# Moving pieces of preparation to other steps and reordering the closing products of a routed attention and GLU kernel

## The chip, the cores and the metric

The kernel runs on one core of one Trainium2 chip. Its five engines work side by side: PE (matmuls), DVE (elementwise work and reductions), ACT (activations), POOL (elementwise work) and SP (which only issues DMAs here). The metric is the device time of one execution in microseconds (us); less is better. All times below are in us unless ns is written.

## The reference, cut to what matters

```python
# 4 batches, 8 heads, 768 tokens, head size 64, 16 centroids per head
q_assign = argmax(q_n @ c_n.T); k_assign = argmax(k_n @ c_n.T)     # nearest centroid
mask = q_assign[:, None] == k_assign[None, :]
attn = softmax(where(mask, q @ k.T / 8, -1e9))
x = (attn @ v) with the heads side by side                         # 3072 x 512
out = (sigmoid(x @ w_gate) * (x @ w_val)) @ w_out                  # 512 -> 1536 -> 512
```

Each query attends only to keys that chose the same centroid. The attention's output goes through a gated feed-forward block.

## The kernel before, in words

**Steps.** The attention runs in 384 steps. A step is one block of 128 keys against 384 queries of one head: one `sc` matmul (line 893), an exponential on ACT (`es`, line 898), and, two steps later for batches 1 to 3, three `av` matmuls (line 916). Batch 1 has steps 96 to 191, batch 2 192 to 287, batch 3 288 to 383. The heads go in pairs, and a pair (b, p) is pair p of batch b. The last pair of a batch is done in two halves of 384 queries: for batch 2 the first half of its last pair takes steps 264 to 275. With it the first 384 tokens of the batch are complete.

**An order written out by hand.** No scheduler moves instructions: each engine executes in the order in which the program issues them. Between the steps, three things are inserted:

- *Feed-forward work* (`ffn_atoms`, line 515, `ffn_run`, line 845): per step as many matmuls as a time budget allows. `g` (line 530) and `v` (line 546) are gate and value products, four matmuls each; `hT` (line 551) on DVE joins them. The output product is made in a Strassen-like form of seven products (`product_out`, line 744). Its matmuls (line 821) alternate between two PSUM banks x and y, and each product's result is added out by DVE (`ob`, line 768) before the bank is used for the next product but one. In order they are known in the trace by their right-hand operands: hT, hT, qheld, kheld, vheld, wo with sum, hT.
- *Preparation of later pairs* (`pair_prep`, line 1451). It splits q and k into high and low halves (`hl`, lines 1458 and 1459), transposes them by DMA (`T<-hl`, line 410), multiplies with the centroids in twelve matmuls (`lg`, line 434), picks the largest on DVE (`lgs`, `mx`, `oh`, lines 449 to 469), transposes the picks by DMA (`ohT`) and copies them into the rows of T that make the mask. `v_sum` (line 324) adds up v over the keys: three adds on DVE (lines 330, 336, 337), a matmul with ones (`vs_ps`, line 341) and a scaling (`sv`, line 346), which the normalisation of the pair needs at its end.
- *Normalisation* (`normalise`, line 366): t and rec on DVE, xp on POOL, then a transposing DMA from SP into `xTb` (line 947), which is the input of `g`.

The table `SCHED` (from line 21) gives the step at which each piece is issued, as an offset to the first step of its pair. `b1p3lg1` is the second head's lg of batch 1, pair 3, whose first step is 168. `b2...` holds for batches 2 and 3 where no `b3p...` entry overrides it: `vs` is the first add of the v sum, `vu` the other two, `vt` the matmul and the scaling, `lg0` and `pk0` the first head's lg and pick. First steps: pair (3,0) 288, pair (3,1) 312.

**PSUM.** The tiles of sc, g, v, lg, vs_ps and o_end take turns in a ring of four banks; a matmul into a bank waits until the bank's former tile has been read.

**The end.** After the last step the second half of batch 3's feed-forward runs alone. `closing` (line 575) makes the output of four blocks of 128 tokens in two such seven-product groups, a and b. `pa(k)` and `pb(k)` are product k of a group, six matmuls of 256 columns (line 594); la and lb are each group's last product. Products 1, 4, 6 and 5 take a bank of their own; product 7 goes on top of 6, and 3 on top of 5, in the same bank, after 6 and 5 have been added out (line 580). For group a these banks are the two fixed output banks, for b ring banks. `last` (line 628) makes the last product in column parts, adds each out, and stores 256 columns of 128 tokens at once (`store`, line 500, on SP's queue).

Of the kernel before, what the change touches and what calls it, by code (L numbers as in the profile page):

```python
# [94 lines left out]
}  # L95


@with_exitstack
def kernel(
# [12 lines left out]
    PE, ACT, DVE, POOL, SP = nc.tensor, nc.scalar, nc.vector, nc.gpsimd, nc.sync  # L112
    B, H, S, D = q.shape
    NCL = centroids.shape[1]
    DM = out.shape[1]
# [45 lines left out]
    def bank(n=512, dt=FP, name="bank"):  # L161
        return ring.tile([128, n], dt, tag="ring", name=name)
# [3 lines left out]
    def out_bank():  # L166
        taken["op"] += 1
        return op.tile([128, DM], FP, tag="o", name="o")
# [94 lines left out]
    HF, HD = NFC // 2, DM // 2  # L263
# [233 lines left out]
    def tok(b, t, f):  # L497
        return HB[b, t // 3][:, HF * f : HF * f + HF, bass.ts(t % 3, 128)]

    def store(src, b, c0, n, m=slice(0, DM)):  # L500
        def f():
            SP.dma_start(
                out=out[b * S : (b + 1) * S].rearrange("(p c) m -> p c m", c=NCH)[
                    :, c0 : c0 + n, m
                ],
                in_=src,
            )

        d_ = SCHED.get("sd", 0)
        if d_ > 0 and b < B - 2:  # L510
            at(step_no[0] + d_, f)
        else:
            f()

    def ffn_atoms(xT, t0, n, b, final=False):
# [55 lines left out]
        if final:  # L571
            return closing(b, gv, sm[(3, 2)], sm[(4, 5)])
        return gv + outs

    def closing(b, gv, ma, mb):

        ac, order = [], []
        plus = lambda dst, a, z: DVE.tensor_tensor(dst, a, z, ALU.add)  # L580

        def pair(m, bk):
            st = {}
            lhs = {
                1: lambda: tok(b, m.t1, 0), 2: lambda: tok(b, m.t1, 1), 4: lambda: tok(b, m.t2, 1),
                6: lambda: m.of[2], 5: lambda: m.of[1], 7: lambda: m.of[3], 3: lambda: m.of[4],
            }
            rhs = {1: B11, 2: B21, 3: B22, 4: T4, 5: T1, 6: T2, 7: T3}
            C = lambda i, j: st["ob"][:, i, HD * j : HD * j + HD]

            def mm(o, k, g, n, start, a=0, z=HD):
                w = lhs[k]()
                for c in range(g, g + n):
                    PE.matmul(  # L594
                        out=o, lhsT=w[:, c, :], rhs=rhs[k][:, c, a:z],
                        start=start and c == 0, stop=c == HF - 1, skip_group_check=True,
                    )

            def product(k, g=0, n=HF):
                def f():  # L600
                    z = {1: "a", 4: "d", 6: "x", 7: "x", 5: "y", 3: "y"}[k]
                    if g == 0 and k in (1, 4, 6, 5):
                        if k == 1:
                            st["ob"] = osp.tile([128, 2, DM], FP, name="ob")
                        st[z] = bk(z)
                    o = st[z][:, 0:HD]
                    mm(o, k, g, n, k not in (7, 3))
                    if g + n < HF:
                        return
                    if k == 1:  # L610
                        ACT.activation(C(0, 0), o, AF.Copy)
                    elif k == 4:
                        plus(C(1, 0), o, C(0, 0))
                    elif k == 6:
                        plus(C(0, 1), o, C(0, 0))
                    elif k == 5:
                        plus(C(1, 1), o, C(0, 0))
                    elif k == 7:
                        plus(C(1, 0), o, C(1, 0))
                        plus(C(1, 1), o, C(1, 1))  # L620
                        store(st["ob"][:, 1:2], b, m.t2, 1)
                    else:
                        plus(C(0, 1), o, C(0, 1))
                        store(st["ob"][:, 0:1, HD:DM], b, m.t1, 1, slice(HD, DM))

                return f

            def last(parts):
                def f():
                    for a, z in parts:  # L630
                        o = bank(z - a, name="o_end")
                        mm(o, 2, 0, HF, True, a, z)
                        plus(st["ob"][:, 0, a:z], o, st["ob"][:, 0, a:z])
                    store(st["ob"][:, 0:1, 0:HD], b, m.t1, 1, slice(0, HD))

                return f

            return product, last

        two = {}  # L640

        def bank_a(z):
            if z in "ad":
                need(*(("wo", i) for i in range(WOP)), *(("wt", i, c) for i in range(4) for c in range(2)))
                two[z] = out_bank()
            return two[{"x": "a", "y": "d"}.get(z, z)]

        pa, la = pair(ma, bank_a)
        pb, lb = pair(mb, lambda z: bank(512, name="o_end"))
        early = [pa(k, g, HF // 2) for k in (1, 4, 6, 5) for g in (0, HF // 2)]  # L650

        def drained(f):
            def g():
                while aside:
                    aside.pop(0)[1]()
                f()

            return g

        early[0] = drained(early[0])  # L660
        atoms = gv[:14]
        for i, x in enumerate(gv[14:]):
            atoms.append(x)
            if i < len(early):
                atoms.append((0.0, early[i]))
        for f in (
            pa(7), pb(1), pb(4), pa(3), pb(6), pb(5), la([(0, HD)]), pb(7), pb(3),
            lb([(0, HD // 2), (HD // 2, HD)]),
        ):
            atoms.append((0.0, f))  # L670
        return atoms
# [280 lines left out]
    def at(i, f):  # L952
        bg.setdefault(max(i, step_no[0] - 0.5), []).append(f)
# [11 lines left out]
    def need(*names):  # L965
        for n in names:
            assert n in done, n
# [361 lines left out]
    a = P[0, 0, 0]  # L1329
# [199 lines left out]
    for b in range(B):  # L1529
        xT = xtp.tile([128, NDC, S], HP, tag="xTb", name="xTb")  # L1530
        key = min(b, 1)
        for i in range(2 if b else NPT):
# [4 lines left out]
            c0, cn = PARTS[i] if b == 0 else (3 * i, 3)  # L1537
            for w in range(1 + (cn > 3)):
                z = cn // (1 + (cn > 3))
# [51 lines left out]
```

## Time and profile before

| what | value |
|---|---|
| median of 3 runs | 322.78 us (322.7 to 324.16) |
| the profiled execution's own time | 323.67 us |
| its span (first to last instruction) | 321.9 us |
| PE's granted clock over the span | 0.999 |
| mean DMA traffic | 140 GB/s |

In a line of the timeline stand the start, the duration, the engine, the line of the kernel, the operation, the output, the input, the shape, and in square brackets how long the engine was idle before and which instruction released it. Lines of the waits give the waiter, the one waited for, the sum, the count and the longest. Lines of the chain give start, duration and the link. SPq and ACTq are the instructions by which SP and ACT issue DMAs; a DMA's line gives its size and the us from issue to landing. Records of matmuls overlap, since each is counted until its data is out.

### The profile page before, as it was taken

What the parts mean: (1) busy time and instruction counts of PE and PEld (TensorE: products, weight loads), DVE (VectorE), ACT (ScalarE), POOL (GpSimd) and SP (SyncE); (2) the same over time, 40 slices, a digit from 0 to 9 for tenths busy, and PEclk for the clock granted to TensorE, in tenths of its full rate; (3) what the DMA queues carried; (4) which work ended last, traced back from release to release, by engine and by line L of the source; (5) the groups of instructions that cost most, each with busy time, mean ns of one, the idle gap of its engine ahead of it and who ended that gap; (6) DMA issues with size and microseconds to landing.
All of it is one profiled execution on the core that took longest, in us unless ns stands there. A gap on an engine that the chain in (4) does not pass through costs nothing.

```text
span 321.9 us, 9181 instructions
## 1 busy us (share of the span) xinstructions
PE 314.6 (98%) x3510; PEld 222.4 (69%) x3510; DVE 224.9 (70%) x598; ACT 231.1 (72%) x521; POOL 108.6 (34%) x145
## 2 busy tenths in 40 slices
PE   7999999999999999999999999999999999999996
PEld 5888666766666666666777687566777688667775
DVE  5799656777787677576878587586767356456666
ACT  6688988787888888877867866778877886332320
POOL 6877464154434365433133333414211111000000
PEclk9999999999999999999999999999999999999999
DMA  7999997738876996978884751942503112200103
GB/s 214 374 256 180 244 171 118 210 75 236 238 113 187 163 238 155 223 172 136 108 219 115 217 113 33 314 110 52 111 2 90 40 26 79 77 2 1 65 2 131
DMA packets 77709, 45.16 MB, mean 140 GB/s; under 512 B 56865, under 2 KB 75105, under 8 KB 77665
## 3 DMA queue, kind: packets, MB, share of 16 engines
q1 hardware_dynamic: 73696, 39.73, 49.7%
q0 software_dynamic: 3680, 4.72, 9.0%
q8 instruction: 27, 0.44, 0.6%
q10 hardware_dynamic: 288, 0.13, 0.2%
q14 instruction: 18, 0.14, 0.2%
HBM read 28.34 MB, written 6.29 MB: 108 GB/s over the span
## 4 chain that ended last, share of the span: by engine, by line
PE 89%; DMA 3%; DVE 3%; issue 2%; POOL 1%; SPq 0%; ACT 0%; POOLq 0%; DVEq 0%
PE g L530 19%; PE v L546 19%; PE sc L893 17%; PE av L916 10%; PE o L821 8%; PE o L684 5%; PE lg L434 2%; PE o_end L594 2%; DMA T<-hl 2%; PE lg L421 1%; PE t_ps L1142 1%; PE o L594 1%; DMA xTb<-xp 1%; PE oh_ps L1202 1%; DMA qraw<-in_q_dram 1%
## 5 line engine op out<-in xcount | busy, mean ns | idle before, releaser
L898 ACT ACTIVATE es<-sc 128x384 f16<-128x384 f32 x384 | 174.3, 492 | 40.6 <-PE sc L893 31.9
L893 PE MATMUL sc<-T 128*128 128x384 f16 x384 | 117.8, 326 | 0.4 <-DVE T L1223 0.4
L916 PEld LDWEIGHTS <-es 128*128 128x128 f16 x1152 | 81.3, 98 | 35.9 <-issue 0.8
L916 PE MATMUL av<-va,es 128*128 128x65 f16 x1152 | 97.6, 194 | 0.0
L551 DVE SCALAR_TENSOR_TENSOR hT<-th,v 128x384 f16<-128x384 f32 x96 | 53.0, 553 | 55.6 <-PE av L916 36.0
L530 PE MATMUL g<-xTb,wg 128*128 128x384 f16 x384 | 78.2, 326 | 0.7 <-DMA xTb<-xp 0.5
L546 PE MATMUL v<-xTb,wv 128*128 128x384 f16 x384 | 78.1, 326 | 0.0
L536 ACT ACTIVATE th<-g 128x384 f32<-128x384 f32 x96 | 47.2, 491 | 35.0 <-PE g L530 15.9
L375 POOL TENSOR_TENSOR xp<-t,rec 128x384 f16<-128x384 f32 (+1 forms) x30 | 21.6, 720 | 101.8 <-DVE rec L372 52.3
L530 PEld LDWEIGHTS <-wg 128*128 128x128 f16 x384 | 37.2, 97 | 19.3 <-issue 0.4
L546 PEld LDWEIGHTS <-wv 128*128 128x128 f16 x384 | 37.4, 98 | 18.6
L893 PEld LDWEIGHTS <-T 128*128 128x128 f16 x384 | 37.1, 97 | 0.6 <-DVE T L1223 0.5
L1459 POOL TENSOR_TENSOR hl<-kraw,hl 128x384 f16<-128x384 f32 x22 | 20.2, 920 | 41.1 <-DVE hl L1458 20.5
L1459 POOL TENSOR_TENSOR hl<-qraw,hl 128x384 f16<-128x384 f32 x22 | 20.9, 950 | 9.8 <-DVE hl L1458 9.8
L768 DVE TENSOR_TENSOR ob<-o,ob 128x256 f32<-128x256 f32 (+1 forms) x35 | 17.8, 523 | 7.6 <-PE o L821 6.8
L370 DVE TENSOR_TENSOR t<-av,sv 128x390 f32<-128x390 f32 (+1 forms) x30 | 14.4, 479 | 9.7 <-PE av L916 7.3
L821 PEld LDWEIGHTS <-sum 128*128 128x128 f16 x168 | 16.4, 98 | 5.2 <-issue 0.8
L684 PE MATMUL o<-wo,hT 128*128 128x512 f16 x72 | 19.9, 379 | 0.0
L821 PE MATMUL o<-wo,hT 128*128 128x256 f16 x126 | 19.8, 272 | 0.0
L449 DVE TENSOR_REDUCE lgs<-lg 128x192 f32<-128x384 f32 x23 | 12.7, 551 | 2.8 <-PE lg L434 2.7
L821 PEld LDWEIGHTS <-hT 128*128 128x128 f16 x126 | 12.2, 97 | 3.4
L322 POOL CAST va<-vraw 128x768 f16<-128x768 f32 x15 | 13.0, 869 | 1.9 <-DMA vraw<-in_v_dram 1.9
(158 smaller groups left out, 340.1 us busy)
## 6 DMA issues: line engine op xcount, KB each, us to landing
vraw<-in_v_dram SPq DMA_DIRECT2D x15, 384.0 KB, 4.9
kraw<-in_k_dram SPq DMA_DIRECT2D x14, 384.0 KB, 4.3
qraw<-in_q_dram SPq DMA_DIRECT2D x12, 384.0 KB, 4.2
out_dram<-ob SPq DMA_DIRECT2D x18, 256.0 KB, 2.4
wg<-in_moe_w_gate_dram POOLq DMA_DIRECT2D x2, 768.0 KB, 9.5
wv<-in_moe_w_val_dram POOLq DMA_DIRECT2D x2, 768.0 KB, 10.3
wo<-in_moe_w_out_dram POOLq DMA_DIRECT2D x2, 768.0 KB, 9.3
T<-ohT SPq DMA_DIRECT2D x44, 24.0 KB, 1.9
```

The source lines that it names most:

```text
L375: (eng or POOL).tensor_tensor(x, t[:, 0:nq, 0:64], bcast(rec[:, 0:nq], 64), ALU.mult)
L530: PE.matmul(out=g[:, 0:n], lhsT=wg[fc // WQ][:, dc, fc % WQ, :], rhs=xT[:, dc, t0 : t0 + n], start=(dc == 0), stop=(dc == NDC - 1),)
L536: ACT.activation(th[:, 0:n], g[:, 0:n], AF.Tanh)
L546: PE.matmul(out=w[:, 0:n], lhsT=wv[fc // WQ][:, dc, fc % WQ, :], rhs=xT[:, dc, t0 : t0 + n], start=(dc == 0), stop=(dc == NDC - 1),)
L551: DVE.scalar_tensor_tensor(HB[b, blk][:, fc, 0:n], st[0][:, 0:n], 1.0, w[:, 0:n], ALU.add, ALU.mult)
L684: PE.matmul(out=o, lhsT=HB[b, blk][:, fc, bass.ts(t, 128)], rhs=wo[fc // WON][:, fc % WON, :], start=(fc == 0), stop=(fc == NFC - 1),)
L768: plus = lambda dst, a, z: DVE.tensor_tensor(dst, a, z, ALU.add)
L821: PE.matmul(out=st[z][:, e], lhsT=a[:, c, :], rhs=rhs[:, c, :], start=start and c + e == 0, stop=c == HF - 1, skip_group_check=True,)
L893: PE.matmul(out=sc.rearrange("p (c t) -> p c t", t=128), lhsT=s["k"], rhs=s["q"], start=True, stop=True,)
L898: ACT.activation(es, sc, AF.Exp, scale=SCALE)
L916: PE.matmul(out=av[:, a0 + s["c0"] + i, :], lhsT=s["es"][:, bass.ts(i, 128)], rhs=VA[b, p][:, e, s["j"], :], start=(first and i == 0 and a ...
L1459: POOL.tensor_tensor(hl[:, :, 64:128], r, hl[:, :, 0:64], ALU.subtract)
```

## The change: five pieces at other steps, another closing order, the last store in two

Pieces of preparation:

| piece | step before | step after |
|---|---|---|
| pair (1,3), second head's lg | 139 | 140 |
| pair (3,0), v sum, first add | 269 | 258 |
| pair (3,0), v sum, other two adds | 271 | 260 |
| pair (3,0), v sum, matmul and scaling | 290 | 279 |
| pair (3,1), first head's lg and pick | 273 | 280 |

In the closing order pb(6), pb(5) and pb(7) go ahead of pa(3) and la. Each column part of a group's last product is stored by itself: for group a there is one part, stored from SP as before; for group b the first 128 columns are stored from SP and the last 128 from ACT's queue.

```diff
-    "b1p3lg1": -29
+    "b1p3lg1": -28
+    "b3p0vs": -30, "b3p0vu": -28, "b3p0vt": -9, "b3p1lg0": -32, "b3p1pk0": -32, "END": 0,
...
-    def store(src, b, c0, n, m=slice(0, DM)):
+    def store(src, b, c0, n, m=slice(0, DM), eng=None):
         def f():
-            SP.dma_start(
+            (eng or SP).dma_start(
...
-                    for a, z in parts:
+                    for a, z, eng in parts:
                         o = bank(z - a, name="o_end")
                         mm(o, 2, 0, HF, True, a, z)
                         plus(st["ob"][:, 0, a:z], o, st["ob"][:, 0, a:z])
-                    store(st["ob"][:, 0:1, 0:HD], b, m.t1, 1, slice(0, HD))
+                        store(st["ob"][:, 0:1, a:z], b, m.t1, 1, slice(a, z), eng)
...
-            pa(7), pb(1), pb(4), pa(3), pb(6), pb(5), la([(0, HD)]), pb(7), pb(3),
-            lb([(0, HD // 2), (HD // 2, HD)]),
+            pa(7), pb(1), pb(4), pb(6), pb(5), pb(7), pa(3), la([(0, HD, SP)]), pb(3),
+            lb([(0, HD // 2, SP), (HD // 2, HD, ACT)]),
```

The key "END" is read nowhere.

2 rows, old and new, of the table SCHED are left out of this document.

## The prediction

> **What bounds the kernel now.** I read the busy times of the page first, then the waits of the PE, then the timeline around each wait, engine by engine, and last the end of the kernel.
>
> ```profile
> PE 314.6 (98%) x3510; PEld 222.4 (69%) x3510; DVE 224.9 (70%) x598; ACT 231.1 (72%) x521; POOL 108.6 (34%) x145
> ```
>
> ```profile
> PE o L821 <- DVE ob L768: 0.6, 1, 0.6
> PE g L530 <- DMA xTb<-xp: 0.5, 1, 0.5
> ```
>
> PE is busy for 314.6 of 321.9 us, and the diff adds and removes no matmul. So only PE's stops can be won or lost, and the tail behind its last matmul. Two of its six waits stand near steps 258 to 290. Each sc matmul is a step; step 273 ends at 192.14, where its lg group stands.
>
> ```profile
> 192.14 0.46 PE L434 MATMUL lg<-cm,T 128*128 128x32 f16 x12
> 192.45 0.32 PE L893 MATMUL sc<-T 128*128 128x384 f16 x1
> ```
>
> ```profile
> 194.68 0.49 PE L821 MATMUL o<-vheld,sum 128*128 128x256 f16 x3
> 195.78 0.49 PE L821 MATMUL o<-wo,sum 128*128 128x256 f16 x3 [0.62 <-DVE ob L768]
> 196.11 0.26 PE L916 MATMUL av<-va,es 128*128 128x65 f16 x3
> ```
>
> ```profile
> 200.48 0.65 PE L530 MATMUL g<-xTb,wg 128*128 128x384 f16 x3
> 201.68 0.32 PE L530 MATMUL g<-xTb,wg 128*128 128x384 f16 x1 [0.54 <-DMA xTb<-xp]
> ```
>
> Records overlap, so I go by starts. Three 256-column matmuls take 0.33 (195.78 to 196.11), 0.109 each. The product on wo,sum could have started at 195.01, so the **first stop** costs 0.77. The g matmuls come every 0.163 (0.65 is two such steps and one full record of 0.32); the fourth was due at 200.97, so the **second stop** costs 0.71.
>
> ```profile
> 192.78 0.26 DVE L336 TENSOR_TENSOR va<-va 128x128 f32<-128x128 f32 x1
> 193.08 0.52 DVE L337 TENSOR_TENSOR vs<-va,va 128x128 f16<-128x128 f32 x1
> 193.52 0.55 DVE L449 TENSOR_REDUCE lgs<-lg 128x192 f32<-128x384 f32 x1
> 194.10 0.35 DVE L460 TENSOR_REDUCE mx<-lgs 128x12 f32<-128x192 f32 x1
> 194.49 0.43 DVE L462 TENSOR_TENSOR oh<-lgs,mx 128x96 f16<-128x96 f32 x2
> 194.95 0.19 DVE L469 TENSOR_SCALAR oh<-oh 128x96 f16<-128x96 f16 x1
> 195.05 1.88 DVE L768 TENSOR_TENSOR ob<-o,ob 128x512 f32<-128x512 f32 x3
> 196.85 0.35 DVE L370 TENSOR_TENSOR t<-av,sv 128x195 f32<-128x195 f32 x1
> ```
>
> This is the cause of the first stop. The first of the three ob adds empties the bank that the wo,sum product reuses. It stands behind the v sums of pair (3,0) (step 271) and the pick of pair (3,1) (step 273), 2.3 us of work. The t behind the adds is the normalisation of the last quarter of batch 2's first half; its result goes through the transpose that the second stop waits for.
>
> ```profile
> 198.06 3.58 DMA xTb<-xp
> ```
>
> **The change part by part.** *Steps 258 to 290.* The v sums go to 258 and 260, the pick and its twelve lg matmuls from 273 to 280. In the built order nothing is left in front of the three adds that DVE has not ended by 192.78. The first add then runs as soon as PE has ended the kheld product, and the whole vheld product, twelve matmuls or 1.31, lies between that and the wo,sum product, against 0.63 for the add: the first stop's 0.77 goes. Its lg group has gone from there too (192.14 to 192.45, 0.31), so the vheld product ends at 194.68 + 0.49 - 0.31 = 194.86. The other two adds follow at 0.6 each (1.88 for three), and t starts at about 196.10 instead of 196.85: 0.75 earlier. From t to the transpose's issue it takes 196.85 to 198.06, 1.21, and 3.58 to its landing. Neither changes, since the SP and POOL orders of this stretch stay as they are. So the fourth g starts at about 200.93. PE itself would be there at 200.97 - 0.77 + 0.06 (the vs_ps matmul, below) = 200.26: the lg group is back in front of it by then. The transpose still ends last, PE still waits 0.67, and **the two stops together give 0.75, not 1.48**.
>
> ```profile
> 206.70 0.22 PE L341 MATMUL vs_ps<-vs,ones 128*128 128x130 f16 x1
> 206.76 0.33 PE L893 MATMUL sc<-T 128*128 128x384 f16 x1
> 206.92 0.26 PE L916 MATMUL av<-va,es 128*128 128x65 f16 x3
> 207.01 0.32 PE L893 MATMUL sc<-T 128*128 128x384 f16 x1
> 207.49 0.81 PE L530 MATMUL g<-xTb,wg 128*128 128x384 f16 x4
> ```
>
> ```profile
> 206.88 0.55 DVE L551 SCALAR_TENSOR_TENSOR hT<-th,v 128x384 f16<-128x384 f32 x1 [0.24 <-PE av L916]
> ```
>
> The sum over the keys (vs_ps) moves from step 290 to 279. It takes one of the four PSUM ring banks, so at 207.49 the g needed the bank that hT emptied at 207.43; it was due at 207.01 + 0.16 = 207.17. Without vs_ps the ring is one place less far on and g takes a bank that an exp has left already. Gain 0.32, and the 0.06 of the matmul itself, which now lies ahead of the second stop where PE waits anyway: **0.38**. At its new place DVE empties its bank behind one ob add, and the ring comes round to it only four tiles, some three steps, later.
>
> ```profile
> 182.75 0.55 DVE L551 SCALAR_TENSOR_TENSOR hT<-th,v 128x384 f16<-128x384 f32 x1 [1.54 <-PE av L916]
> ```
>
> ```profile
> 184.63 0.33 PE L893 MATMUL sc<-T 128*128 128x384 f16 x1
> ```
>
> At 258 and 260 the v sums stand by the first of these rows: the first add, 384 columns like the hT's 0.55, in the 1.54 us in which DVE was idle, the other two (0.26 and 0.52 above) between this hT and the next lgs. That lgs (0.55) then ends at 183.30 + 0.78 + 0.55 = 184.63 at the latest, just when the sc of the second row wants its bank. I cost this at nothing, since records on DVE overlap a little; with the cover gone it is up to those 0.78.
>
> *Step 139 to 140.*
>
> ```profile
> 94.51 4.85 DMA T<-hl
> ```
>
> ```profile
> 99.02 0.26 PE L916 MATMUL av<-va,es 128*128 128x65 f16 x3
> 99.41 0.47 PE L434 MATMUL lg<-cm,T 128*128 128x32 f16 x12
> ```
>
> The transpose lands at 99.36 and lg starts at 99.41; it was due 0.09 behind the av (206.92 to 207.01), at 99.11, so it costs 0.30. One step on, an sc and an av (206.76 to 207.01, 0.25) go ahead of it and it is due at 99.36. **Gain 0.25**, bounds 0 and 0.30. The pick of this group stands at step 141 and does not care.
>
> *The closing products.* pb(7) accumulates on the bank of pb(6), so its first matmul waits until DVE has added out pb(6); the built order has that wait. Before, pb(5) and la stood between the two; now only pb(5).
>
> ```profile
> 314.71 0.75 DVE L580 TENSOR_TENSOR ob<-o,ob 128x256 f32<-128x256 f32 x2
> 315.38 0.41 DVE L580 TENSOR_TENSOR ob<-o_end,ob 128x256 f32<-128x256 f32 x1
> 315.71 0.41 DVE L580 TENSOR_TENSOR ob<-o,ob 128x256 f32<-128x256 f32 x1
> ```
>
> ```profile
> 313.94 0.28 PE L594 MATMUL o_end<-wo,hT 128*128 128x256 f16 x1
> ```
>
> DVE is behind here: it does pa(7)'s two adds and pb(4)'s, and only then, in the place where pa(3)'s add stands at 315.71, pb(6)'s. That ends at 316.12, and PE starts 0.05 later (as 207.43 to 207.49). PE, however, has done the last matmul of pb(4) (313.94) and twelve of pb(6) and pb(5) by 313.94 + 13 x 0.109 = 315.36. **A new stop of 0.81**, with pa(3), la and pb(3) queued behind it on PE, though they need nothing from it. Behind it come as many matmuls as before, so PE's end and the last add move by 0.81. Bounds: 0, if the adds ran as PE delivers, and 1.1, if the four of them took a full 0.41 each with no overlap.
>
> The Trainium skill, "TensorE: Matmul & The Clock Gate", section "Step-by-step: what each phase is for", says that matmuls stay in program order and only weight loads are pulled ahead. By that rule nothing overtakes pb(7). The trace agrees: in the first stop the av at 196.11, which needs nothing from the ob add, came behind the waiting product. If a later matmul could go ahead, pa(3) would fill 0.65 of the 0.81.
>
> ```profile
> 317.99 0.83 PE L594 MATMUL o_end<-wo,hT 128*128 128x128 f16 x12
> 318.86 0.29 DVE L580 TENSOR_TENSOR ob<-o_end,ob 128x128 f32<-128x128 f32 x1
> ```
>
> ```profile
> 319.23 0.40 SPq L502 DMA_DIRECT2D out_dram<-ob  x1
> ```
>
> ```profile
> out_dram<-ob SPq DMA_DIRECT2D x1, 128.0 KB, 1.8
> ```
>
> ```profile
> kraw<-in_k_dram ACTq DMA_DIRECT2D x1, 96.0 KB, 2.6
> ```
>
> *The last store.* Now one store of 128 KB goes out 0.08 behind the last add. Then its first half goes ahead on SP, and 64 KB go out from ACT, which is idle. No wait on SP is saved (0.08 is the wake-up), so only the size counts. Bounds: the 1.8 of 128 KB shrinks by half to 0.9 at the very best (-0.9), or it is like the 2.6 of the one ACT transfer of about that size, a load at the start (+0.8). I take -0.1, by the nearest row, the last store itself. The Trainium skill, "DMA: Bandwidth & Descriptors", section "Rules for kernel authors", speaks against this part: spreading DMAs over issuing engines gives no bandwidth, only the sequencer's issue time. By the same page's fit, given for GpSimd's path ("Anatomy of one DMA"), of 2 us plus bytes over 436 GB/s, the half size would save 0.15 (an estimate); the sum by that is 0.05 lower. The trace agrees as far as it goes, since SP issues at once.
>
> **Sum:** -0.25 - 0.75 - 0.38 + 0.81 - 0.10 = -0.67 us. The profiled execution took 323.67 (span 321.9 and 1.8 around it), the median of the runs is 322.78; taken off both, 323.0 and **322.1**.
>
> **The rivals.** *No stop at pb(7)* (the DVE adds keep up, or the wait falls elsewhere): -1.48, 321.3. For it: the records of the adds overlap (0.75 for two of 0.41), so DVE may do them closer together than their starts show. Against it: these starts are 0.33 apart with their operands long there, and the order is fixed.
>
> *The transpose does not move, and the tail still costs.* If its landing at 201.64 hangs on the DMA engines rather than on t, all that is won before it, 0.25 and 0.75, is waited away; -0.38 + 0.81 - 0.10 = **+0.33, 323.1, slower than before**. It acts in full if t to landing takes 1.0 longer than 1.21 + 3.58; from 0.67 of such a delay on, the change is slower than before. For it: 3.58 is long beside its issue time; against: its chain back to t has no other wait.
>
> *More comes than I see:* the v sums at 258 stall the ring (+0.8) and the ACT store takes 2.6 (+0.9 on my term): 322.1 + 1.7 = 323.8; with the second rival 324.8. Or no stop and a store at 0.9: 320.5.
>
> **How the numbers follow.** Forecast 0.58, no stop 0.16, transpose stays 0.16, both store and ring bad (or worse) 0.06, better than all 0.04. The range takes in the first three with their spread and leaves most of the last two out: 321.0 to 323.6. Over 0.5% (1.6 us, about what a measurement of this kernel can tell from no change) is below 321.2 or above 324.4: faster 0.04 and half of the no-stop case with its store, 0.12; slower 0.06 with spread, 0.07; the rest, 0.81, the same.
>
> **What would show it.** Right: the wait of o L821 on the ob add gone; g L530 still waiting for xTb, 0.5 to 0.7; no gap at the g behind step 290; lg of step 140 without a wait; a new PE wait at o_end of 0.6 to 0.8 for the DVE add, some 3 us ahead of the last matmul. Wrong: that last wait missing, a fourth g not earlier, an sc waiting for DVE around 184, or the last store landing more than 2 us behind its issue.

## The result and the profile after

| what | before | after |
|---|---|---|
| median, 20 runs each | 323.24 us (322.42 to 324.24) | 324.02 us (323.13 to 325.75) |
| the profiled execution's own time | 323.67 | 323.9 |
| its span | 321.9 | 322.1 |
| its first sc of step 256 | 178.40 | 178.18 |

The ratio is 1.0023, 95% interval 1.0012 to 1.0034: the change costs about 0.75 us (0.39 to 1.10), where the prediction had a gain of 0.67 and a range up to 323.6. Lines of the kernel after are one higher than before, from the added row of the table on.

The waits of PE in the kernel after (waiter, the one waited for, sum, count, longest):

```profile
PE g L531 <- DMA xTb<-xp: 0.7, 1, 0.7
PE o_end L595 <- DVE ob L581: 0.6, 1, 0.6
```

Against the rows of before, the wait of the o product for the ob add is gone, that of g for xTb is still there, and a wait in the closing products is new. All three were forecast. Now each place in the timeline of after, beginning with step 140:

```profile
99.37 0.26 PE L917 MATMUL av<-va,es 128*128 128x65 f16 x3
99.46 0.46 PE L435 MATMUL lg<-cm,T 128*128 128x32 f16 x12
```

lg follows the av by 0.09, so its wait of 0.30 is gone. Then the two stops near steps 273 to 284:

```profile
194.39 0.49 PE L822 MATMUL o<-vheld,sum 128*128 128x256 f16 x3
194.72 0.49 PE L822 MATMUL o<-wo,sum 128*128 128x256 f16 x3
```

```profile
196.12 0.35 DVE L371 TENSOR_TENSOR t<-av,sv 128x195 f32<-128x195 f32 x1
```

```profile
197.34 1.20 SPq L948 DMA_TRANSPOSE xTb<-xp  x1
199.77 0.65 PE L531 MATMUL g<-xTb,wg 128*128 128x384 f16 x3
201.16 0.32 PE L531 MATMUL g<-xTb,wg 128*128 128x384 f16 x1 [0.73 <-DMA xTb<-xp]
```

The product on wo,sum comes 0.33 behind the three before it, so the first stop is gone. Counted from step 256 (178.40 and 178.18, the table above), t starts at 17.94 instead of 18.45 and the transpose is issued 0.50 earlier. But the fourth g is due at 199.77 + 3 x 0.163 = 200.26 and starts at 201.16: the second stop is 0.90, where it was 0.71. From the issue to that g it takes 3.82, before 3.62.

The stop that was not forecast stands in front of step 264:

```profile
183.32 0.30 DVE L338 TENSOR_TENSOR vs<-va,va 128x128 f16<-128x128 f32 x1
183.37 0.49 ACT L537 ACTIVATE th<-g 128x384 f32<-128x384 f32 x1 [0.16 <-PE g L531]
183.51 0.33 PE L894 MATMUL sc<-T 128*128 128x384 f16 x1
183.53 0.55 DVE L450 TENSOR_REDUCE lgs<-lg 128x192 f32<-128x384 f32 x1
183.91 0.81 PE L547 MATMUL v<-xTb,wv 128*128 128x384 f16 x4
184.65 0.33 PE L894 MATMUL sc<-T 128*128 128x384 f16 x1
```

v should follow the sc of 183.51 by 0.16, at 183.67. It starts at 183.91, when th has ended (183.86): 0.24 late, and the sc of step 264 behind it stands 6.47 after step 256 instead of 6.23. Behind step 290 and at the end:

```profile
206.44 0.32 PE L894 MATMUL sc<-T 128*128 128x384 f16 x1
206.60 0.81 PE L531 MATMUL g<-xTb,wg 128*128 128x384 f16 x4
```

```profile
313.83 0.75 DVE L581 TENSOR_TENSOR ob<-o,ob 128x256 f32<-128x256 f32 x2
313.83 0.82 PE L595 MATMUL o_end<-kheld,sum 128*128 128x256 f16 x6
314.49 1.08 DVE L581 TENSOR_TENSOR ob<-o_end,ob 128x256 f32<-128x256 f32 x3
315.29 0.81 PE L595 MATMUL o_end<-vheld,sum 128*128 128x256 f16 x6 [0.64 <-DVE ob L581]
```

```profile
318.45 0.62 DVE L581 TENSOR_TENSOR ob<-o_end,ob 128x128 f32<-128x128 f32 x2
318.56 0.81 SPq L503 DMA_DIRECT2D out_dram<-ob  x2
319.15 0.35 ACTq L503 DMA_DIRECT2D out_dram<-ob  x1
```

g follows its sc by 0.16: no gap. pb(7) starts at 315.29, where PE had its turn at 313.83 + 6 x 0.109 = 314.48: a stop of 0.81. The last add ends at 319.07 and ACT issues the store 0.08 later, as SP did.

Last, the end of SP. Here it waits for the semaphores of the DMAs, and its first DRAIN starts when the last of these waits is over. The waits of SP in the last stretch and the row of its DRAINs (ns least, mean, most; first and last start), before:

```profile
SPq L1586 <- DMA out_dram<-ob: 0.9, 3, 0.4
```

```profile
L1586 SPq DRAIN  x3: 7/7/7, 321.1 to 321.4; - x3
```

and after:

```profile
SPq L1587 <- DMA out_dram<-ob: 1.4, 1, 1.4
```

```profile
L1587 SPq DRAIN  x3: 7/7/7, 321.3 to 321.6; - x3
```

Before, SP waited three times and for 0.4 at most; after, once, for 1.4. In the order that was built SP ends with one wait for each of eight semaphores, always in the same order, and the DMAs from SP and ACT take these semaphores in turn. The last store of before took the eighth, so the other waits passed while it flew. One more DMA gives the last store of after the first, and the seven other waits come behind its landing.

### The profile page after: what moved, and what is told of

Its sections match the earlier page's. It is cut to its first block, busy times and chain, and to the rows that moved or that the text cites. A ratio compares the mean times of both kernels' runs of the same rounds, so it can differ in the third digit from the quotient of the medians.

```text
span 322.1 us, 9184 instructions
## 1 busy us (share of the span) xinstructions
PE 314.6 (98%) x3510; PEld 222.2 (69%) x3510; DVE 225.4 (70%) x598; ACT 231.3 (72%) x521; POOL 108.6 (34%) x145
## 4 chain that ended last, share of the span: by engine, by line
PE 87%; DVE 6%; issue 3%; POOL 1%; DMA 1%; ACT 1%; ACTq 0%; POOLq 0%; DVEq 0%
PE g L531 19%; PE v L547 19%; PE sc L894 18%; PE av L917 10%; PE o L822 7%; PE o L685 5%; PE lg L435 2%; PE lg L422 1%; DMA xTb<-xp 1%; PE t_ps L1143 1%; PE oh_ps L1203 1%; PE o L595 1%; PE o_end L595 1%; DVE ob L581 1%; DVE hT L552 1%
## 5 line engine op out<-in xcount | busy, mean ns | idle before, releaser
L1460 POOL TENSOR_TENSOR hl<-qraw,hl 128x384 f16<-128x384 f32 x22 | 20.9, 950 | 10.3 <-DVE hl L1459 10.3
```

Of the source, the lines that this page charges most:

```text
L1460: POOL.tensor_tensor(hl[:, :, 64:128], r, hl[:, :, 0:64], ALU.subtract)
```

## The experiments

Times are against the kernel before on the same chip; "us" is the ratio less one, times 323.3, with the ends of its interval.

| kernel | what it is | ratio (95%) | us |
|---|---|---|---|
| mid | the five moved pieces alone | 0.9989 (0.9977 to 1.0002) | -0.36 (-0.74 to 0.06) |
| order | the closing order alone | 1.0020 (1.0006 to 1.0033) | +0.65 (0.19 to 1.07) |
| act | last store in two, second half from ACT | 1.0038 (1.0022 to 1.0055) | +1.23 (0.71 to 1.78) |
| close | order and act | 1.0054 (1.0033 to 1.0074) | +1.75 (1.07 to 2.39) |
| split_sp | last store in two, both from SP | 1.0015 (1.0 to 1.003) | +0.48 (0 to 0.97) |
| act_whole | last store whole, from ACT | 1.0018 (1.0006 to 1.003) | +0.58 (0.19 to 0.97) |
| one_more | another store in two, in mid kernel | 1.0015 (1.0 to 1.0029) | +0.48 (0 to 0.94) |
| pa3 | closing order with pa(3) ahead of pb(7) | 0.9993 (0.9978 to 1.0007) | -0.23 (-0.71 to 0.23) |
| mid_again | as mid, other chip | 0.9981 (0.9963 to 1.0) | -0.61 (-1.20 to 0) |
| mid_vu29 | mid, two v adds at 259, not 260 | 0.9965 (0.9946 to 0.9984) | -1.13 (-1.75 to -0.52) |
| after_sp | after, second half from SP | 1.0019 (1.0002 to 1.0035) | +0.61 (0.06 to 1.13) |
| mid_pa3 | mid_vu29 and pa3 | 0.9971 (0.9956 to 0.9985) | -0.94 (-1.42 to -0.48) |
| before_shift | before, 57 small matmuls more at the start | 0.9985 (0.997 to 0.9999) | -0.48 (-0.97 to -0.03) |
| after_shift | after, the same | 0.9994 (0.998 to 1.0007) | -0.19 (-0.65 to 0.23) |
| mid29_shift | mid_vu29, the same | 0.9947 (0.9928 to 0.9965) | -1.71 (-2.33 to -1.13) |
| midpa3_shift | mid_pa3, the same | 0.9943 (0.9925 to 0.9961) | -1.84 (-2.42 to -1.26) |

### The change in its parts: mid, order, act, close

```diff
mid:
-    -40.0, "b1p3lg1": -29, "b1p3pk1": -27.0, ...
+    -40.0, "b1p3lg1": -28, "b1p3pk1": -27.0, ...
+    "b3p0vs": -30, "b3p0vu": -28, "b3p0vt": -9, "b3p1lg0": -32, "b3p1pk0": -32,
order:
-            pa(7), pb(1), pb(4), pa(3), pb(6), pb(5), la([(0, HD)]), pb(7), pb(3),
+            pa(7), pb(1), pb(4), pb(6), pb(5), pb(7), pa(3), la([(0, HD)]), pb(3),
act (with the edits of store and last in the change):
-            lb([(0, HD // 2), (HD // 2, HD)]),
+            lb([(0, HD // 2, SP), (HD // 2, HD, ACT)]),
```

> Only the pieces of preparation are moved (the five of the table); the closing and the last store are as before. Theory 1 (the two profiles show all of it): the g behind step 291 starts 0.9 us earlier and nothing is given back, so 0.9 us or 0.3% faster than before. Rival (the moves gain little in most executions, and the profile of before was one in which the transposes landed late): 0.0 to 0.3 us faster. In the profile both want no PE wait of o L821 for DVE; theory 1 wants PE's last matmul 0.8 to 1.0 us earlier than before's.

> Only the closing order; the last store is one of 128 KB from SP as before. Theory 1: the stop of 0.8 us ahead of pb(7) alone, 0.8 us or 0.25% slower, and the time from the last add to the end of the span as before (2.75 us). Rival (the stop is made up elsewhere, since the adds of pb(7) no longer stand late): below 0.4 us slower.

> Only the split of the last store, its second half from ACT; the closing order is as before. Theory 1: the store lands 0.2 us earlier, but at the end SP waits for the DMA semaphores one after the other, and the ACT store now has the first of them, so the other waits come behind its landing: 0.2 us slower, with 0.5 us instead of 0.1 from landing to SP's drain. Rival as predicted: 0.1 us faster. Other rival: a store from ACT lands as late as the load at the start, 2.6 us, 0.8 us slower.

> Only the closing order and the split last store (second half from ACT); the pieces of preparation are at their old steps. Theory 1: a PE stop of 0.8 us ahead of pb(7), and 0.2 us from the last store, 1.0 us or 0.3% slower than before. Rival: 0.7 to 0.8 us slower, all of what the whole change costs, with the moves worth nothing.

The moved pieces gain 0.36 instead of 1.38, the order costs 0.65, as the stop of 0.8 said, and the store costs 1.23 where -0.1 was forecast. close is the sum of order and act (1.88) within its interval. So the order's stop fits, and two terms are wrong: the store and the moved pieces.

### The last store: split_sp, act_whole, one_more, after_sp

```diff
split_sp:  + lb([(0, HD // 2, SP), (HD // 2, HD, SP)])
act_whole (last hands ACT on to store):
-            lb([(0, HD // 2), (HD // 2, HD)]),
+            lb([(0, HD // 2), (HD // 2, HD)], ACT),
one_more (store of batch 0):
-                    store(ob, b, 3 * blk + t, 1)
+                    if (blk, t) == (1, 2):
+                        store(ob[:, 0:HD], b, 3 * blk + t, 1, slice(0, HD))
+                        store(ob[:, HD:DM], b, 3 * blk + t, 1, slice(HD, DM))
+                    else:
+                        store(ob, b, 3 * blk + t, 1)
after_sp (on the kernel after):
-            lb([(0, HD // 2, SP), (HD // 2, HD, ACT)]),
+            lb([(0, HD // 2, SP), (HD // 2, HD, SP)]),
```

> The kernel before with only the last store split in its two column halves, both issued from SP; before alone was 323.38 in the last set of runs, the same split with the second half on ACT 324.44 (+1.23). Theory A (half rows land late and vary, 1.6 to 2.6 us for 64 KB against 1.8 for 128 KB in one, and SP's chain of waits at the end starts with the semaphore of the last store): the queue of the second half does not matter, so +0.8 to +1.4, with SP's long wait of 1.5 us or more as the first of its chain at the end. Rival B (ACT's queue is what is slow): SP issues the second half as it issued the whole, so 0 to +0.3. Rival C (only the order of the waits costs): +0.4 to +0.5, with both halves landed by 1.8.

> The kernel before with its last store whole, 128 KB, but issued from ACT; the number of DMAs is that of before, so the chain of waits at SP's end keeps its order. Theory A (the size of the rows and the order of the waits): 0 to +0.2. Rival B (ACT's queue is slow): +0.6 to +1.2, the landing 2.4 us or more behind the issue. Rival C (order of the waits alone): 0.

> The kernel before with one store of batch 0, in the middle of the kernel, split in its two halves of 256 columns; the last store is as before, but one DMA more has gone out, so its semaphore is the first in the chain of waits at SP's end and no longer the last. Theory C (the order of the waits costs about 0.45, since the other waits then come behind the landing instead of beside its flight): +0.35 to +0.5, the first drain of SP 0.5 behind the landing where it was 0.1. Rival (the chain's order costs nothing, and what the change lost there is in the stores alone): 0, within 0.1.

> The changed kernel with the second half of its last store from SP instead of ACT. Theory J (ACT's queue costs about 0.5 only where ACT issues 0.37 behind the last add, as in act, close and act_whole; the profile of the changed kernel has it 0.08 behind): no gain over the changed kernel, +0.6 to +0.8 over the kernel before. Rival K (the ACT queue costs 0.4 to 0.6 in the changed kernel too): +0.1 to +0.4. In both the semaphore of the last store is the first of SP's waits at the end, as in the changed kernel.

Read from the traces (rows of the last DVE add, the last issue, the DMA packets and SP's first DRAIN; in us). before, one_more, split_sp, act_whole and act have the old closing order, the other four the new one:

```
             add's end   issue to      last packet      sum
             to issue    last packet   to first DRAIN
before         0.08         1.41           0.43         1.92
one_more       0.08         1.42           0.87         2.36
order          0.06         1.32           0.43         1.82
after          0.08         1.28           0.86         2.22
after_sp       0.40         1.25           0.86         2.51
split_sp       0.56         1.25           0.86         2.67
act_whole      0.37         1.68           0.53         2.58
close          0.37         1.37           1.06         2.80
act            0.36         1.94           0.90         3.19
```

Against before, the sums of one_more, split_sp, act_whole and act are longer by 0.44, 0.75, 0.66 and 1.27; the runs have 0.48, 0.48, 0.58 and 1.23. one_more changes nothing at the end but the place of the last store's semaphore. Its waits of SP and the DRAINs, with the landing otherwise as before:

```profile
SPq L1590 <- DMA out_dram<-ob: 1.4, 1, 1.4
```

```profile
L1590 SPq DRAIN  x3: 7/7/7, 320.8 to 321.1; - x3
```

The one long wait of after is there, 0.87 instead of 0.43 lie between the last packet and the DRAIN, and the time rises by 0.48 (0 to 0.94): **in the trace the order of the waits alone costs 0.44.**

The half size has to be compared within one closing order, since the whole store alone lands 0.09 earlier in the new one (1.41 in before, 1.32 in order; the cause is open). In the old order half the size saves 0.16 (1.41 to 1.25 in split_sp), in the new one only 0.04 and 0.07 (1.32 to 1.28 in after and 1.25 in after_sp). By the fit of the Trainium skill, "DMA: Bandwidth & Descriptors", section "Anatomy of one DMA", given for GpSimd's path, it would save 0.15 (an estimate). The old order agrees, the new one does not.

From SP the second half goes out late instead, 0.40 and 0.56 behind the add, since SP is still busy with issuing what stands before it (0.4 each); so ACT's queue has its use. But in act, act_whole and close ACT issues 0.37 behind the add, against 0.08 in after, and in act and act_whole the last packet is late besides. after_sp takes the same as after, within the intervals: in the changed kernel ACT's queue is not what costs. In split_sp theory A's +0.8 did not come; in act_whole the +0.58 is more than theory A allowed.

Nor is the queue what makes act's packets late. There the half from SP is as late as that from ACT (last packet 1.96 behind its issue, in split_sp and after_sp 1.25), and it is the half from SP that has the first of SP's waits, not the one from ACT. In those three kernels an 8 KB instruction load on queue 14 comes 0.6 to 0.9 behind the issue, in after it is over 7 us earlier. In act it takes 319.28 to 319.90. Of the 128 packets of each half, 120 have ended by 319.40 and 319.62, and the last eight, a sixteenth, follow from 319.90 and 320.10 on. In act_whole the last eight start when the load ends, at 320.48. So the late packets stand behind the load in the traces; no run moved that load. Why ACT issues 0.3 later in these three is open.

### The closing order: pa3

```diff
-            pa(7), pb(1), pb(4), pa(3), pb(6), pb(5), la([(0, HD)]), pb(7), pb(3),
+            pa(7), pb(1), pb(4), pb(6), pb(5), pa(3), pb(7), la([(0, HD)]), pb(3),
```

> The kernel before with the closing order pa(7), pb(1), pb(4), pb(6), pb(5), pa(3), pb(7), la, pb(3): the new order but with pa(3) back in front of pb(7). The last store is single and on SP. Theory D (the order's whole +0.65 is the stop of 0.8 that pb(7) makes with the DVE adds): pa(3)'s six matmuls fill 0.65 of it, so a stop of 0.15 and +0.1 to +0.2. Rival E (the new order costs by something else, such as the banks or the adds of la and pb(3) at the end): the stop goes and the time stays, +0.5 or more.

```profile
314.79 0.82 PE L594 MATMUL o<-wo,T 128*128 128x256 f16 x6
315.60 0.82 PE L594 MATMUL o_end<-vheld,sum 128*128 128x256 f16 x6
```

The six matmuls of pa(3) fill the stop: pb(7) comes 0.81 behind them instead of 0.66, a stop of 0.15. And order's +0.65 becomes -0.23, not to be told from nothing, though the intervals of the two touch (0.19 and 0.23). In the traces the stop of 0.81 is the only place where the order costs; the tail behind the last add is even 0.10 shorter with it (1.82 for 1.92 in the table).

### The moved pieces: mid_vu29, mid_again, mid_pa3

```diff
mid_vu29, on mid:
-    "b3p0vs": -30, "b3p0vu": -28, "b3p0vt": -9, ...
+    "b3p0vs": -30, "b3p0vu": -29, "b3p0vt": -9, ...
```

> The five moved pieces alone (closing products and last store as in the kernel before), but with the other two v adds of pair (3,0) at step 259 instead of 260. Theory F (in the change these two adds stand between an hT and the lgs at step 260; lgs ends later, v and sc exchange their banks of the ring in the built order, v waits for th, and step 264 starts 0.23 late): at 259 the two adds run in the DVE idle time ahead of that hT, the built order gives v and sc their old banks, so the 0.23 at step 264 is gone and the time is 0.2 below that of the pieces as in the change (mid_again). Rival G (the 0.23 comes from the add at 258 or from ACT): step 264 keeps its delay, and both take the same.

> The five moved pieces alone once more, with the closing order and the last store of the kernel before, beside the others on this chip: the first set gave 0.9989 (-0.36 us, interval -0.7 to +0.1). Theory H (step 140 gives 0.2 on the mean of several profiles of the old middle, step 264 costs 0.23, the two stops near steps 278 to 285 give 0.5, the sum over the keys 0.31): -0.5 to -1.0 where the transpose lands as before. Rival I (the transpose of xTb does not come earlier, its landing simply varies by 0.8 from run to run and takes back all that is won in front of it): -0.3.

> What the runs so far point to as the fastest: the five moved pieces with the two v adds at 259, the closing order with pa(3) between pb(5) and pb(7), and the single last store from SP as before, so that its semaphore stays the last of SP's waits. If the parts add up: -0.6 from the pieces and -0.2 to +0.15 from the order, so -0.4 to -0.8 against the kernel before.

The semaphores that the instructions wait for name the cause at step 264. Before, v waited for lgs and the sc behind it for th; with the v adds in front of lgs the two tiles have exchanged their banks, and v waits for th, which ends later. With the adds a step earlier the banks are as they were, and DVE does both adds in its idle time ahead of hT (line 552). mid_vu29, DVE:

```profile
181.78 0.91 DVE L338 TENSOR_TENSOR vs<-va,va 128x128 f16<-128x128 f32 x1
182.62 0.55 DVE L552 SCALAR_TENSOR_TENSOR hT<-th,v 128x384 f16<-128x384 f32 x1
183.09 0.55 DVE L450 TENSOR_REDUCE lgs<-lg 128x192 f32<-128x384 f32 x1
```

and PE:

```profile
183.60 0.33 PE L894 MATMUL sc<-T 128*128 128x384 f16 x1
183.76 0.81 PE L547 MATMUL v<-xTb,wv 128*128 128x384 f16 x4
```

v follows by 0.16 again, step 264 stands at 6.23 behind step 256, and the time is 0.5 below mid_again's, though the two intervals overlap. Theory F holds in the trace. But mid_again and mid together are worth 0.5, still far from 1.38, and in mid_vu29's profile, with the transpose issued 0.73 earlier than before, g still waits for it, longer than ever:

```profile
PE g L531 <- DMA xTb<-xp: 1.1, 1, 1.1
```

### The transpose and PE's own instructions: before_shift, after_shift, mid29_shift, midpa3_shift

The kernel's eight profiles with the old middle (before, close, order, act, split_sp, act_whole, one_more, pa3) give the second stop as 0.71, 0.41, 0.64, 0.31, 0.25, 0.28, 0.29 and 0.15, mean 0.38; the six with moved pieces (mid, after, mid_again, after_sp, mid_vu29, mid_pa3) as 0.43, 0.90, 0.72, 0.90, 1.24 and 0.61, mean 0.80. The transpose is issued 0.50 to 0.73 earlier, and most of that is waited away. In the packets of the trace (us behind the issue; the transpose has 384 packets of 256 bytes, 24 for each of 16 DMA engines):

```
             PE's 16 KB load   90% of the    last      fourth g
             on one engine     packets by    packet    starts
pa3           0.40 to 1.42        1.63        2.11       3.06
before        1.24 to 2.16        1.61        2.85       3.62
after         1.04 to 2.37        1.62        3.06       3.82
mid_vu29      1.73 to 2.61        1.63        3.30       4.16
after_shift   none                1.59        1.70       2.92
```

One DMA engine is taken for 0.9 to 1.5 us (over the fourteen profiles) by a load of PE's own instructions, and that engine's share of the transpose comes behind it. The trace does not name the engines; that it is one engine is read from the packets. In the six profiles with moved pieces exactly 24 of the 384 packets end later than 1.75, and in after the first of these starts at 2.35, where the load ends at 2.37. In all fourteen the last packet comes 0.51 to 0.70 behind the end of the load, and the fourth g 0.76 to 0.96 behind that. One thing stays open: in mid_vu29 the 24 had not begun when the load's record starts at 1.73, though all the others were done at 1.72. The load comes at 20.0 to 20.9 behind step 256 in all fourteen profiles, whether the transpose is early or late. The DMA view of the kernel after, from the issue of the transpose to the fourth g (packets, MB, share of 16 engines):

```profile
q1 hardware_dynamic: 507, 0.28, 27.1%
q8 instruction: 1, 0.02, 2.2%
```

2.2% of 16 engines in 3.82 us is 1.34: that one packet. And over the whole execution:

```profile
q8 instruction: 27, 0.44, 0.6%
```

27 loads of 16 KB for PE's 3510 matmuls and 3510 weight loads, one for every 256 or so. The Trainium skill, "Advanced Engine Details and Errata", section "ISA Cache", has a line of 16 KB or 256 instructions; the trace agrees. By the Trainium skill, "DMA: Bandwidth & Descriptors", section "Queues, rings and completion order", a DMA engine ends a packet before it turns to another ring. The trace agrees, with the 2.35 and 2.37 of after.

To test it, the loads were moved. The warm-up matmuls at the start, whose results nothing reads, were cut in pieces, the 21 of 128 columns in three of 42 and the five of 512 in four, so that every later load comes 57 matmuls earlier:

```diff
-                PE.matmul(out=w[:, 0:m], lhsT=warm[:, 0:128], rhs=warm[:, 0:m], ...)
+                n, w2 = (4, 128) if m == 512 else (3, 42)
+                for j in range(n):
+                    PE.matmul(out=w[:, 0:w2], lhsT=warm[:, 0:128], rhs=warm[:, 0:w2], ...)
```

> The kernel before, with the 21 warm-up matmuls of 128 columns ahead of the first steps cut into three of 42 columns and the five of 512 into four of 128: 57 matmuls more in about the same time, so that each of PE's later 16 KB instruction loads comes 57 matmuls (some 5 us) earlier against the steps. Theory L (the transpose into xTb behind step 284 is held by the load that PE's own instructions take over one of the 16 DMA engines; without a load there its last packet ends 1.64 behind the issue, as 90 of 100 packets do in all 14 profiles, and g starts 0.77 behind that): the fourth g is not stopped, against a mean of 0.4 in eight profiles of the old middle: -0.4 here, if no other transpose is hit in its place. Rival M (the landing varies by itself, by the memory or by the stores behind it): the lag from the issue of the transpose to the fourth g stays between 3.1 and 4.2, and the time within 0.2.

> The changed kernel with the same cut warm-up matmuls. Theory L: the transposes lag falls from 3.8 to 2.4, the fourth g is not stopped, 0.7 to 0.9 less than the changed kernel, so about 0 against the kernel before. Rival M: as the changed kernel, +0.7.

> The five moved pieces with the two v adds at 259, and the cut warm-up matmuls; closing and last store as before. Theory L: the fourth g starts at 21.85 behind step 256 instead of 22.45 and 23.08 in two profiles, so 0.6 to 1.2 below the kernel without the cut: -1.6 to -2.2 against the kernel before. Rival M: -1.1, as without the cut.

> The same with pa(3) between pb(5) and pb(7) in the closing order, the fastest if the parts add up. Theory L: -1.4 to -2.2 against the kernel before. Rival M: -0.9, as without the cut.

after_shift, the timeline and the DMA view of the same stretch:

```profile
197.17 1.20 SPq L948 DMA_TRANSPOSE xTb<-xp  x1
199.61 0.81 PE L531 MATMUL g<-xTb,wg 128*128 128x384 f16 x4
```

```profile
q1 hardware_dynamic: 533, 0.34, 36.0%
```

No load, no stop: the four g run in one piece, in all four shift kernels, and the last packet ends 1.70 or 1.71 behind the issue in all four. after_shift takes 0.94 less than after by the ratios (give or take some 0.6, by the two intervals), the size of after's second stop (0.90); before_shift 0.48 less than before, for 0.38 of the mean stop and the wait of the lg at step 139 (0.21 in the mean), which is gone there too. Theory L holds, rival M falls. mid29_shift against before_shift is -1.23: with the load out of the way, the moved pieces are worth what is won in front of the transpose. The traces have 0.73 of it at the fourth g and 0.37 at the sum over the keys. The loads then fall elsewhere: midpa3_shift's profile has a wait of lg for a T<-hl transpose of 0.7 at step 188 that the other three do not have; there PE's load takes 1.9, in the others 1.2 to 1.3.

mid29_shift and midpa3_shift, at 321.58 and 321.37 with 323.34 for before beside them, beat both kernels.

## Why the prediction was wrong, point by point

- **Step 139 to 140** (-0.25): right. 0.30 between the two profiles, 0.21 on the mean of the eight old middles; none of the six moved ones waits there for more than 0.1.
- **The v sums at 258 and 260** (nothing): the step failed. The prediction saw that lgs would end "just when the sc of the second row wants its bank" and relied on overlap. The bank was another one: the late lgs makes v and sc exchange banks, v waits for th, and 0.23 is lost ahead of everything that follows. mid_vu29 takes it away. It also makes t 0.51 earlier instead of 0.75.
- **The first stop** (0.77 goes): right; 0.78 is gone in every moved kernel.
- **"From t to the transpose's issue it takes 1.21, and 3.58 to its landing. Neither changes"**: this is the step that failed most. 1.21 held (196.12 to 197.34, 1.22). The 3.58 was not a constant: it was 1.70 to the last packet as without a load, 1.15 of wait behind PE's instruction load, and 0.73 from the last packet to the landing. The load keeps its place among PE's instructions and not beside the transpose; 3.06 to 3.62 to the fourth g in eight profiles, 3.35 to 4.16 in the moved ones. So the second rival, that the landing hangs on the DMA engines and not on t, had the mechanism: the two stops together gave 0.30 between the two profiles, with the 0.23 above in it, and 0.75 was forecast. On the means of the eight old middles and of the four with the adds at 260, the fourth g came 0.13 earlier. What the rival had too high is the price: the gain at step 140 was kept.
- **The sum over the keys** (-0.38): right; 0.31 at step 293 in every moved kernel and the 0.06 of the matmul itself.
- **The closing order** (+0.81): right, 0.81 in the profile, with cause and place. Nothing overtook pb(7). order's run has +0.65 (0.19 to 1.07).
- **The last store** (-0.10): a wrong sign. The step that failed is "No wait on SP is saved (0.08 is the wake-up), so only the size counts". It left out that the split makes one DMA more, and that SP's waits at the end have an order: +0.43. The last store of before had the best place of the eight. Between the two profiles the last packet came 0.13 earlier, but 0.09 of it belong to the closing order and only 0.04 to the size.

In the pair of profiled executions the terms are: moved pieces -0.97 for -1.38, the stop +0.81 for +0.81, the tail +0.30 for -0.10, and 0.09 more ahead of step 96, where the two kernels have the same instructions; +0.23 in all, as the spans say (322.1 and 321.9). On the means the moved pieces are worth 0.21 at step 139, 0.13 at the fourth g and 0.37 at the sum over the keys, 0.71 together; mid and mid_again measured 0.36 and 0.61. What the 0.75 has beyond the 0.23 is in the choice of the base: the profiled execution of before lies 0.43 above its median (its second stop of 0.71 is 0.33 above the mean), and that of after 0.12 below. And the base of the forecast, 322.78 from three runs, was low: 20 runs of before have 323.24, so 0.46 of the distance between 322.1 and 324.02 is no mistake about the change. A sum taken from one execution also counts as won the waits that most executions do not have.

## What to carry to other kernels

Before a transfer's flight time is carried over to an earlier issue, see in the DMA view what else its engines carried: a load of instructions takes one of sixteen engines for a microsecond, and a transpose that uses all sixteen lands behind it. Count the DMAs in front of the last store: with a chain of waits in fixed order at the end, one more of them can cost as much (0.43 here) as the stop in the middle that one is hunting. And before a stop is priced, look at more than one execution: here the wait for xTb was 0.15 to 0.71 in eight profiles whose instructions up to there are the same.

## What the runs showed of the hardware that was not expected

- PE's instructions come in loads of 16 KB, each 0.9 to 1.9 us on one DMA engine in the places looked at, beside the kernel's own transfers. 57 small matmuls more at the start made the kernel before faster by 0.48 (0.03 to 0.97); in its profile the two waits behind such transposes (0.38 and 0.21 in the mean) are gone.
- SP's waits at the end cost 0.43 between the last packet and the first DRAIN where the last store's semaphore is the last waited for, and 0.86 where it is the first, as long as no instruction load falls beside the store (0.53 and 0.90 to 1.06 where one does).
- 64 KB in rows of half the length had their last packet 1.25 to 1.28 behind the issue in after, split_sp and after_sp, 1.37 in close and 1.94 in act. In act the last eight of 128 packets on either queue follow an 8 KB instruction load of 0.62.
